# A recurrent attention kernel and its feed-forward: weight loads behind the last crossbar transposes, and the last segment's transposes on TensorE

## The chip, the cores and the metric

The kernel runs on one core of a Trainium2 chip. The time is device microseconds of one launch, as the median of ten runs. Beside the times there is one profiled execution, whose trace all profile lines below are taken from. Engines are called PE (TensorE matmul), PEld (TensorE weight load), DVE (VectorE), ACT (ScalarE), POOL (GpSimd) and SP (SyncE). POOL and SP compute little here: they issue most of the transfers, each in its own order.

## The reference

Two parts follow each other. Part A is attention with a recurrent memory: 2048 tokens in 64 segments of 32, 32 heads of 128, and 8 memory tokens whose output in one segment is the memory of the next. Part B is a gated feed-forward layer on the sum.

```
x = A_x                                   # (1, 2048, 640)
mem = mem0                                # (1, 8, 640)
for s in range(64):
    h = concat([mem, layernorm(x)[segment s]])        # 40 rows
    q, k, v = h @ Wq, h @ Wk, h @ Wv                  # 32 heads x 128
    p = softmax(mask(q k^T * 128**-0.5))              # causal, memory always seen
    o = (p v) @ Wo
    mem, outs[s] = o[:8], o[8:]
h  = x + concat(outs)
n  = layernorm(h)
h2 = h + (relu(n @ W_gate) * (n @ W_up)) @ W_down     # 640 -> 1728 -> 640
```

Because of `mem`, the segments of part A cannot be reordered. In the last segment the memory queries are not needed, since no later segment uses its memory.

## The kernel before, in words

The program is a list of operations, each with its engine, the keys it reads and the keys it writes. `G.solve()` turns keys into semaphore waits; each engine then runs its own operations in the order in which they were added. So the order of the calls is the order of work on every engine, and there is no scheduler. `("Wdone", j)` is written by every projection with weight j (0 for Q, 1 for K, 2 for V), so a load that reads this key starts only after the last such projection.

**A segment.** The loop at L874 runs over s. `project` (L402) multiplies the segment's 32 activations with 4096 columns of a weight in 5 chunks of 128, two halves and four column groups, 40 matmuls of 512 columns. Eight of the 32 columns are the memory; the other 24 are *riders*, tokens of later segments whose keys, queries and values are projected early and kept in the rings Kr, Qr and Vr. A projection arrives with tokens and heads spread over partitions, `to_tok` copies it to bf16 (half on ACT, half on DVE), and a crossbar transpose on SP's queue (`dma_t`, L359) turns it for use: KS (L901) for keys, QS (`trans_q`, L453) for queries. `evac_k` and `evac_q` then copy the riders into the rings, and `v_riders` (L487) moves theirs to Vr with small transfers on POOL's queue. The memory queries alone are needed at once, and TensorE picks them out with eight small matmuls (`pick_mem`, L444).

Then come `scores` (L554), the exponents `exp_mem` and `exp_x` on ACT, the masks on DVE, and the memory rows' product with V (`pv_mem`). `norm_om` and `trans_om` give oT, `wo_pass` (L630) multiplies by Wo in 128 matmuls of 160 columns, and `to_act` puts the new memory into the next segment's activations. This is the recurrence. Between its steps `filler` puts extra riders' projections (`extra_units`, L827) or every fourth segment's collected output rows (`woe_pass`, L643). Segment 1 and segment 62 have neither.

The other 32 rows' output takes a second path: `pv_x` and `norm_x` (L664, L683) write ox, and in the *next* segment `trans_ox` (L693) transposes it by crossbar into oT. Of its rows, 24 share the 32-wide `wo_pass` with the memory of that segment, and 8 are copied to oTe (`copy_oTe`, L697) for `woe_pass`. `rows` and `store_attn` write results to attn_d in memory.

**The seam.** The SBUF of the projection weights W is used again for the feed-forward. In segment 62, right after the Q projection, `load_gate_up` (L815) issues five transfers on POOL: xn2T (the first block's normalised activations), Wg and Wu of 2080 KB each, and two pieces of 80 KB. The last segment leaves the loop after its V projection (L927 to L929). The code from L1050 then issues h and Wd on POOL and eight row loads on SP (`ln2_load`, L713), and mixes segment 63's remaining attention with the first four units of the feed-forward:

```
gate_up(0, 0); scores(s); exp_x(); copy_oTe(s - 1); mask_x()
gate_up(0, 1); pv_x(s, P0); norm_x(P0); wo_pass(T1); rows(T1, 0, s - 1); trans_ox()
gate_up(0, 2); gate_up(0, 3); copy_oTe(s); wo_pass(P2); rows(P2, 1, s); woe_pass(P3, range(16))
```

`gate_up(b, j)` (L995) is one unit: 5 matmuls with Wg and 5 with Wu, 512 tokens wide, relu on ACT, the product on DVE. There are 14 units for each of four blocks, then `down`. From j=5 of block 0 on, DVE also does the layer norm of the next block (`ln2_front`, L718), which needs the rows that SP loaded.

## Time and profile before

| what | value |
|---|---|
| median of ten runs | 1131.71 us (1129.3 to 1138.39) |
| profiled execution | 1133.65 us |
| its span in the trace | 1131.9 us |
| PE busy | 1069.5 us (94%) |
| PEld / DVE / ACT / POOL busy | 509.2 / 592.9 / 352.9 / 288.0 us |
| mean granted PE clock | 0.983 |
| segment 62 | 897.21 to 916.77 us |
| segment 63 and units j=0 to 3 | 916.77 to 955.81 us |
| rest of the feed-forward | 955.81 to 1131.9 us |

The span is the time from the first to the last instruction in the trace. The execution's own time is a little longer, and the median of the ten runs is a little below that execution. In the lines of slices each digit is a fortieth of the span: 9 means 90% busy or more, and in the clock's row 9 is close to full clock. In timelines the first number is the start, the second the duration, then engine, line of the source, operation, output and inputs; in brackets stands how long the engine was idle before and what released it. "To landing" is the time from the issue of a transfer until its data has arrived.

### The profile page before, as it was taken

How to read it: one execution, taken by the hardware profiler on the slowest of the kernel's cores; microseconds unless marked ns; L12 is line 12 of the kernel's file. 1: busy time of each engine (PE TensorE's matmuls, PEld its weight loads, DVE VectorE, ACT ScalarE, POOL GpSimd, SP SyncE). 2: the span in 40 equal slices, each digit the busy share in tenths (PEclk: the TensorE clock that was granted, in tenths of full speed). 3: DMA queues.
4: the chain of work that ended last, by engine and by line, in shares of the span. 5: the costliest groups of instructions: out<-in, count | busy, mean ns of one | idle time of the engine just before them, and what ended most of it. 6: DMA issues, size and time to landing. Idle time of an engine off the chain costs nothing.

```text
span 1131.9 us, 55578 instructions
## 1 busy us (share of the span) xinstructions
PE 1069.5 (94%) x28030; PEld 509.2 (45%) x23471; DVE 592.9 (52%) x1477; ACT 352.9 (31%) x729; POOL 288.0 (25%) x575
## 2 busy tenths in 40 slices
PE   5579999999999999999999999999999958999998
PEld 3344444454444444444444454444444534343443
DVE  3245656565655555666566566555555522553522
ACT  2113333333333333333324333333333311221211
POOL 1013333332323232424242424333332420000000
PEclk9979999999999999999999999999999978999999
DMA  9936464646454455665655666464546484122100
GB/s 354 378 79 109 92 103 88 109 80 110 81 104 89 98 95 99 102 118 112 114 100 115 110 107 101 89 102 84 104 88 103 86 252 123 38 79 73 27 18 24
DMA packets 291880, 122.66 MB, mean 108 GB/s; under 512 B 268064, under 2 KB 281280, under 8 KB 291648
## 3 DMA queue, kind: packets, MB, share of 16 engines
q1 hardware_dynamic: 272272, 95.21, 40.9%
q0 software_dynamic: 19184, 23.89, 9.5%
q8 instruction: 202, 3.31, 1.2%
q14 instruction: 30, 0.25, 0.1%
q10 hardware_dynamic: 192, 0.01, 0.0%
HBM read 36.79 MB, written 7.21 MB: 39 GB/s over the span
## 4 chain that ended last, share of the span: by engine, by line
PE 84%; DMA 8%; DVE 3%; SPq 3%; issue 1%; ACT 0%; DVEq 0%; ACTq 0%
PE ps L419 24%; PE ps L397 23%; PE ps L636 13%; PE ps L1005 10%; PE ps L1038 3%; PE ps L564 3%; PE ps L650 3%; SPq L357 3%; DMA Wo<-in_A_Wo_dram 3%; PE ps L601 3%; DMA QS<-tok 2%; DVE TBf L548 2%; PE ps L448 2%; DMA oT<-ox 1%; DMA Kr<-tok 1%; PE ps L616 1%
## 5 line engine op out<-in xcount | busy, mean ns | idle before, releaser
L419 PE MATMUL ps<-W,act_r 128*32 128x512 bf16 x4277 | 398.5, 386 | 15.2 <-DMA W<-in_A_Wq_dram 3.1
L397 PE MATMUL ps<-W,act_r 128*32 128x512 bf16 x3603 | 353.7, 379 | 0.0
L357 POOL DMA_DIRECT2D Vr<-Vp x376 | 188.4, 508 | 453.0 <-ACT Vp L459 279.5
L419 PEld LDWEIGHTS ps<-W,act_r 128*32 128x32 bf16 x4277 | 117.3, 98 | 274.5 <-issue 214.7
L459 ACT ACTIVATE tok<-ps 128x512 bf16<-128x512 f32 x191 | 110.5, 595 | 253.6 <-PE ps L397 222.9
L636 PE MATMUL ps<-Wo,oT 128*32 128x160 bf16 x8320 | 163.3, 238 | 9.0 <-DMA Wo<-in_A_Wo_dram 7.4
L461 DVE CAST tok<-ps 128x512 bf16<-128x512 f32 x131 | 90.6, 691 | 146.9 <-PE ps L397 121.9
L636 PEld LDWEIGHTS ps<-Wo,oT 128*32 128x32 bf16 x8320 | 148.7, 99 | 35.2 <-DVE oT L461 25.7
L419 PE MATMUL ps<-W,act_e 128*32 128x512 bf16 x900 | 90.5, 381 | 0.0
L397 PE MATMUL ps<-W,act_e 128*32 128x512 bf16 x900 | 90.1, 379 | 0.0
L459 ACT ACTIVATE Qr<-QS 128x512 bf16<-128x512 bf16 (+3 forms) x108 | 70.7, 681 | 52.6 <-DMA QS<-tok 52.4
L689 DVE TENSOR_TENSOR ox<-ps,rx 128x512 bf16<-128x512 f32 x128 | 82.4, 685 | 2.2
L357 POOL DMA_DIRECT2D attn_d<-wtok x64 | 46.7, 729 | 143.0 <-ACT wtok L459 143.0
L548 DVE STREAM_TRANSPOSE TBf<-ps 128x160 f32<-128x160 f32 x64 | 22.4, 350 | 96.5 <-PE ps L636 96.4
L1005 PE MATMUL ps<-xn2T,Wg 128*128 128x512 bf16 x260 | 66.4, 387 | 3.3 <-ACT tok L459 3.3
L1020 DVE TENSOR_TENSOR hT<-g,ps 128x512 bf16<-128x512 bf16 (+1 forms) x56 | 38.5, 687 | 53.7 <-PE ps L1005 49.8
L1005 PE MATMUL ps<-xn2T,Wu 128*128 128x512 bf16 x260 | 66.3, 387 | 0.0
L574 ACT ACTIVATE om<-ps 128x128 bf16<-128x128 f32 x63 | 17.5, 278 | 147.8 <-PE ps L564 147.8
L1038 PE MATMUL ps<-Wd,hT 128*128 128x320 bf16 (+1 forms) x240 | 63.3, 300 | 0.0
L461 DVE CAST Vp<-ps 128x512 bf16<-128x512 f32 x64 | 44.3, 692 | 34.0 <-PE ps L397 23.5
L1018 ACT ACTIVATE g<-ps 128x512 bf16<-128x512 f32 (+1 forms) x56 | 32.5, 593 | 93.4 <-PE ps L1005 93.3
L397 PE MATMUL ps<-Wd,hT 128*128 128x320 bf16 x208 | 56.9, 299 | 0.0
(104 smaller groups left out, 1145.5 us busy)
## 6 DMA issues: line engine op xcount, KB each, us to landing
Vr<-Vp POOLq DMA_DIRECT2D x124, 48.8 KB, 1.9
W<-in_A_Wk_dram SPq DMA_DIRECT2D x2, 2560.0 KB, 13.3
W<-in_A_Wq_dram SPq DMA_DIRECT2D x2, 2560.0 KB, 28.4
W<-in_A_Wv_dram SPq DMA_DIRECT2D x2, 2560.0 KB, 27.4
Wo<-in_A_Wo_dram SPq DMA_DIRECT2D x2, 2560.0 KB, 27.4
xt<-in_A_x_dram SPq DMA_DIRECT2D x30, 160.0 KB, 3.6
Vr<-Vp POOLq DMA_DIRECT2D x128, 32.5 KB, 1.9
attn_d<-wtok POOLq DMA_DIRECT2D x64, 40.0 KB, 2.8
```

The costliest lines, as they stand in the source:

```text
L357: add(eng, lambda e: e.dma_start(dst, src), r=r, w=w, dma=True)
L397: return pe.add_instruction(mybir.InstMatmult(name=nc.get_next_instruction_name(), engine=mybir.EngineType.PE, ins=[pe.lower_ap(rhs), pe.l ...
L419: ins = pe.matmul(*a, start=(c == 0), stop=(c == DC - 1), skip_group_check=True)
L459: add("act", lambda a: a.activation(dst, src, ACTF.Copy), r=r, w=w)
L461: add("dve", lambda v: v.tensor_copy(dst, src), r=r, w=w)
L548: add("dve", lambda v: v.transpose(TBf[:].rearrange("p c t -> p (c t)"), src), r=[wkey], w=[("TBf",)])
L564: i = pe.matmul(bank((P0, P1)[g % 2])[p:p + (M if a else 32), 40 * k:40 * k + 40], lh, Qr[:, h, q, :], start=True, stop=True, skip_group_c ...
L636: i = pe.matmul(bank(bk)[32 * gg:32 * gg + 32, 0:160], oT[:, hb, :], w[:, gg], start=(hb == ORDER[0]), stop=(hb == ORDER[31]), skip_group_ ...
L689: add("dve", lambda v, kh=kh: v.tensor_tensor(ox[:, :, kh, :], src[:, :, kh, 0:128], ap(rx, kh, [[2, 4], [0, 128]]), ALU.mult), r=[B(b0 + ...
L1005: ins = pe.matmul(bank(bk), w[:, c, lo:lo + 128], xn2T[par][:, c, :], start=(c == 0), stop=(c == DC - 1))
L1020: add("dve", lambda v: v.tensor_tensor(hT[par][lo:128, j, :], g1[gi][lo:128, :], bank(bu)[lo:128, :], ALU.mult), r=[B(bu), ("g1", gi)], w= ...
L1038: i = pe.matmul(*a, start=(j == 0), stop=(j == FC - 1), skip_group_check=True)
```

## The change

There are three edits, all between segment 62 and the feed-forward.

1. `load_gate_up` takes a further key. It is called in segment 62 after `copy_oTe(61)` and reads that copy's key, so that POOL waits until the last oT transpose of the loop has landed and been copied. `v_riders` of segment 62 now stands ahead of it on POOL's queue. The row loads and h also read `("Wu",)`.
2. In segment 62 the queries are not transposed by crossbar. `trans8` does eight 128x128 transposes on TensorE, DVE copies the memory queries from PSUM, and ACT the riders' queries.
3. The last segment leaves the loop. Its keys are transposed by `trans8`; ox of segments 62 and 63 by a new `trans_pe` (two groups of four transposes, copied by ACT and DVE), the former into QS, which is free, the latter into oT. The output product of segment 62 reads QS in two halves. The four units `gate_up(0, 0..3)` come after all attention work, and the row loads, h and Wd are issued near the end of it.

```diff
+    def trans_pe(dst, keys):
+        flat = ox[:].rearrange("p k g d -> p (k g d)")
+        for n, (b, eng) in enumerate(((T0, "act"), (T1, "dve"))):
+            def f(pe, n=n, b=b):
+                for k in range(4):
+                    o = 512 * n + 128 * k
+                    ins = pe.matmul(bank_bf(b)[:, k * 128:(k + 1) * 128], flat[:, o:o + 128], ident[:, :],
+                                    is_transpose=True)
+                return ins
+            add("pe", f, r=[("ox", 0), ("ox", 1), ("ident",)], w=[B(b)])
+            copy_op(eng, dst[:, 16 * n:16 * n + 16, :], slots(b, 0, 32)[:, 0:16, :], [B(b)], keys)
...
     def ln2_load(i):
         u = i % 4
-        dma(xt2[u][:, :], x_ap[128 * i:128 * i + 128, :], r=[("Wdone", 1)], w=[("xt2", u)])
-        load_attn(at2[u], i, [("Wdone", 1)], ("at2", u))
+        dma(xt2[u][:, :], x_ap[128 * i:128 * i + 128, :], r=[("Wdone", 1), ("Wu",)], w=[("xt2", u)])
+        load_attn(at2[u], i, [("Wdone", 1), ("Wu",)], ("at2", u))
...
-    def load_gate_up():
-        free = [("Wdone", 0)]
+    def load_gate_up(after):
+        free = [("Wdone", 0)] + after
...
+            if last:
+                break
...
-                if s == NSEG - 2:
-                    load_gate_up()
...
-                if nr:
-                    trans_q()
+            if nr and s < NSEG - 2:
+                trans_q()
             loads()
             project(a, ks, 2, (0, 1), (P2, P3), (0, 1), spare=16)
-            if not last:
+            if s == NSEG - 2:
+                trans8(tok[2], ("tok", 2), tok[3], ("tok", 3), T0)
+                copy_op("dve", Qr[:, :, q, 0:M], slots(T0, 0, M), [B(T0)], [("Qm", q)])
+                evac_q(slots(T0, 0, SEG), B(T0), t0, nr, M, "act")
+            else:
                 pick_mem(T0)
...
             copy_oTe(s - 1)
+        if s == NSEG - 2:
+            load_gate_up([("oTe", (s - 1) % 4)])
         norm_om()
...
+    a, ks = pass_act(s)
+    project(a, ks, 2, (0, 1), (P2, P3), (0, 1))
+    trans8(tok[0], ("tok", 0), tok[1], ("tok", 1), BQ[0])
+    copy_op("dve", KS[:, :, 0:M], slots(BQ[0], 0, M), [B(BQ[0])], [("KS",)])
+    project(a, ks, 2, (0, 1), (P2, P3), (2, 3))
+    scores(s)
+    project(a, ks, 2, (0, 1), (P2, P3), (4,))
+    exp_x()
+    to_v(P3, Vp, 1, ("Vp",), "dve")
+    to_v(P2, Vp, 0, ("Vp",), "act")
+    mask_x()
+    trans_pe(QS, [("QS",)])
+    pv_x(s, P0)
+    copy_op("act", oTe[:, :, M * ((s - 1) % 4):M * ((s - 1) % 4) + M], QS[:, :, 0:M], [("QS",)], [("oTe", (s - 1) % 4)])
+    norm_x(P0)
+    wo_pass(BQ[1], None, QS, [("QS",)], (0,))
+    trans_pe(oT, [("oT", "m"), ("oT", "x")])
+    wo_pass(BQ[1], None, QS, [("QS",)], (1,))
+    rows(BQ[1], 0, s - 1)
+    copy_oTe(s)
+    for i in range(4, 8):
+        ln2_load(i)
+    dma(h_rows[0] <- h_d, waits Wdone 1 and Wu, eng="pool")
+    dma(Wd <- B_W_down, two pieces, waits Wdone 1, eng="pool")
+    wo_pass(BQ[0])
+    rows(BQ[0], 1, s)
     woe_pass(P3, range(16))
     woe_sum(P3)
     woe_store(NSEG // 4 - 1)
+    for j in range(4):
+        gate_up(0, j)
```

The removed lines of the last segment are those quoted in the section on the kernel before. The two `dma(... <- ...)` lines are shortened; the transfers are those of before. `wo_pass` gets arguments for its source, its keys and which of its halves to run.

## The prediction

> **What bounds the kernel now.** I read the slices of the span first.

> ```profile
> PE   5579999999999999999999999999999958999998
> PEclk9979999999999999999999999999999978999999
> ```

> A slice is 28.3 us. TensorE is full from the fifth slice to the end but for slices 33 and 34 (906 to 962 us), where its clock drops too. That is the seam between the last two segments and the feed-forward part, and all edits lie there. The chain of waits over it, merged:

> ```profile
> 903.67 20.67 DMA QS<-tok
> ...
> 927.03 13.65 DMA oT<-ox
> ...
> 943.01 3.94 PE ps L636 x106
> 946.95 4.42 PE ps L1005 x20
> ...
> 955.88 20.61 PE ps L1005 x95
> ```

> Two crossbar transposes hold the end: 34.3 us. From 955.8 on the chain is feed-forward matmuls back to back, and stays so to 1131.9. So the span is the start of the feed-forward's unit j=4 (955.81 in the timeline) plus a tail of 176.1 us. Why the transposes are late shows in POOL's timeline and in the landing times of tile oT, earlier (first landing line, 830 to 900 us) and at the seam (second, 900 to 950 us):

> ```profile
> 902.01 0.59 POOL L357 DMA_DIRECT2D xn2T<-xn_d  x1 [3.11 <-PE ps L397]
> 902.60 0.90 POOL L357 DMA_DIRECT2D Wg<-in_B_W_gate_dram  x1
> 904.32 0.88 POOL L357 DMA_DIRECT2D Wu<-in_B_W_up_dram  x1
> 906.02 2.03 POOL L357 DMA_DIRECT2D Vr<-Vp  x4
> ```
> ```profile
> DMA to landing us min/median/max: 2.8/2.8/2.8
> ```
> ```profile
> DMA to landing us min/median/max: 8.0/10.9/13.7
> ```

> The same transpose lands in 2.8 us when the DMA engines are free and in 8.0 and 13.7 us beside 5 MB of weights. QS, issued at 903.67, took 20.7. The windows show what TensorE does meanwhile (busy time, count; then granted clock, DMA share, GB/s):

> ```profile
> 905.00:910.00 5.00, 0.55 (x16) 0.27 (x16) 0.53 (x3) 1.17 (x3) 3.05 (x6) 0.88 1.06 323
> 910.00:915.00 5.00, 3.44 (x100) 3.17 (x104) 1.95 (x6) 0.00 (x0) 0.00 (x0) 0.50 1.04 320
> 935.00:940.00 5.00, 1.35 (x4) 0.30 (x2) 0.00 (x0) 0.00 (x0) 0.00 (x0) 0.84 1.12 265
> ```

> **Segment 62.** In before it runs from 897.21 to 916.77, where segment 63's first projection starts. Removed: the QS transpose (1 DMA, and 3.51 us of SP's queue). Moved: the five loads of xn2T, Wg, Wu and Wgu, now behind the copy of oT to oTe, behind the four rider DMAs on POOL. Added: eight 128x128 transposes in place of eight 128x32 picks (0.30 us). The opening's transposes took 0.90 us per 16 at full clock, so 0.45: +0.15. ACT's copy of the queries (0.63) moves from behind the QS landing to about 903.1, into ACT's idle time ahead of the exponent at 904.92; nothing is charged, and if it collided it would cost its 0.6. Scores then end at 904.85.

> With no weights in flight the oT transpose, issued at 902.28, lands at 905.1 (2.8), before DVE reaches the copy at about 905.9. Its wait of 4.63 us goes. What is late next is the latency chain exp, mask, memory product, norm, transpose, output product. No filler work exists in segment 62, so I need a segment that also has none: segment 1.

> ```profile
> 74.63 0.28 PE L616 MATMUL ps<-ident,om 128*128 128x128 bf16 x2 [0.73 <-DVE om L609]
> 75.29 3.90 PE L636 MATMUL ps<-Wo,oT 128*32 128x160 bf16 x128 [0.38 <-DVE oT L461]
> 79.86 0.40 PE L419 MATMUL ps<-W,act_r 128*32 128x512 bf16 x4
> ```

> Its scores end at 72.45 and segment 2 starts at 79.86: 7.4 us. So segment 63 starts at S = 904.85 + 7.45 = 912.3 instead of 916.77: 4.5 us won.

> Here the clock matters: that output product took 3.90 us, against 2.32 in a filled segment. [...] I take the row.

> **Segment 63.** Before, it takes 916.77 to 955.81, 39.04 us, of which 8.64 are the units j=0 to 3 (four of 2.16). After, those units follow the attention work, so attention must run with nothing in the gaps. All KS and ox transposes go to TensorE; no DMA is left on the chain. Worked from S:
> K projection 40 matmuls at 0.054, 2.16. DVE's half of the token copy ends at S+3.08 (916.77 to 919.16, plus 0.69); V chunks 0 and 1 (0.86) cover it. Eight transposes 0.45 to S+3.6. KS copy on DVE, 0.2 latency and 0.29, S+4.1, covered by V chunks 2 and 3 to S+4.46; uncovered it would cost 0.5. Scores 0.6, S+5.06. V chunk 4 and the first ox transposes (0.43, 0.45) cover part of exp (0.60, ends S+5.9). DVE's V copy 0.69 ends at S+6.4, the two masks 1.02 (911.83 to 912.85) at S+7.42. Product with V, then DVE's reciprocal at S+8.15 and norm 0.24 + 1.29, S+9.7. The first half of segment 62's output product (half of 2.32) hides there. Transposes 0.45 with 0.05 latency, S+10.2; second half 1.15; segment 63's output product 2.3; the oTe product 2.3: S+15.95. The PSUM copies (a 512-element one: about 0.42 on DVE, between its rows of 0.29 and 0.69 for 256 and 1024; 0.6 on ACT) run beside the second half-product.

> At half clock from S+7.45 to the warm-up, the product, both half-products and the last transposes add 1.85 by the same steps. TensorE is busy some 70% of S+3.6 to S+9.2 against under half in segment 1's gaps, so this is uncertain: between 0 and 1.85 I take 1.2, nearer segment 1. Gate j=0 starts at G = 912.3 + 15.95 + 1.2 = 929.45; segment 63 takes 17.15 without the units against 30.4: 13.25 won.

> **The weights, now later.** POOL waits for the copy (906), but the riders, which wait for ACT's V copy (905.7), occupy it until 907.9, so the added wait costs nothing. The five loads are 5.08 MB; at the 320 GB/s of the windows 15.9 us, so from first bytes near 909.5 to 925.4. Upper end: before's whole duration, 902.01 to 922.8, again from 907.9: 928.7. Both are before Wu is needed at G+1.08. Behind them on POOL stands segment 61's attention store; ACT's copy of wtok for segment 62 must wait for its landing, about 925.5, while due at S+12.5 = 924.8. ACT next frees bank 0 for gate j=0 near 927.6, so this is covered by the oTe product to 929; a landing past 928.5 would move G one for one. The h and Wd loads and SP's eight row loads now wait behind Wu or ACT: 4.1 MB from about 927, 13 us, done by 940. The first row is needed by DVE at j=5 (943), Wd at 960. Before they landed in 7 to 12 us of contention. Instruction fetch beside the weights cost TensorE one stall (0.77 us at 920.1); 0 to 1, inside the range.

> **Sum.** 1131.9 - 4.5 - 13.25 = 1114.15 us of span (929.45 + 8.64 + 176.1 = 1114.2). The profiled execution took 1133.65, 1.75 above its span, and the median is 1131.71, 1.94 below it. The median after: 1114.2 + 1.75 - 1.94 = 1114.0.

> **Rivals.** *Clock stays full* through both segments: 1114.0 - 1.6 - 1.2 = 1111.2. [...]
> *Clock stays low* from the scores of 63 to the gate: about 8.6 us of TensorE work from S+5 on doubles, some 3 of it under DVE's waits: +5.6 in place of 1.2, 1118.4. Against it: after 4 us of work the clock returned at 916.
> *Weights or the store take the place of the transposes.* Wu or the store landing at 932 to 937 would start the gate there: 1116 to 1122. Against it: 320 GB/s held for 15 us and nothing large competes now.
> *Slower:* Wd is now issued after an attention store and h, some 2 us after 926; the first down product, near 960, waits on it. From a landing at 981 on, 54 us after issue, the kernel is slower by 0.3%; against: 11.9 us today.
> *The change does nothing:* only if oT still lands late without the weights; 2.8 us in every earlier segment speaks against.

> **How the numbers follow.** Likeliest case 60%, full clock 15%, low clock 12%, weights or store 8%, slower 4%, nothing 1%. The likeliest alone spans 1112 to 1116.5. The range, 1110.5 to 1119, takes in both clock cases and the first half of the weights case. A measurement tells about 0.3% (3.4 us) from no change: faster 0.95, same 0.01, slower 0.04.

> **What would show it.** Right: no DMA wait over 1 us on the chain between 897 and the gate; segment 63 starting near 912.3; an output product of about 3.9 us in segment 62; POOL's Wg issue near 908.5; the gate near 929.5; a tail of 176 us from j=4. Wrong: TensorE waiting at the gate on Wu, on ACT's wtok copy, or DVE on the attention rows at j=5; or a half clock beyond 920.

## The result, and the profile after

| | before | after |
|---|---|---|
| median | 1131.87 us (1128.3 to 1138.39, 32 runs) | 1118.14 us (1116.44 to 1120.95, 9 runs) |
| after / before | | 0.988, 95% interval 0.9864 to 0.9896 |
| profiled execution, its span | 1133.65, 1131.9 us | 1120.42, 1118.7 us |
| segment 62 starts | 897.21 | 898.49 |
| segment 62 lasts | 19.57 | 13.66 |
| segment 63 to the start of unit j=4 | 39.03 | 30.42 |
| from j=4 to the end | 176.1 | 176.1 |

Forecast were 1114.0 us and a range from 1110.5 to 1119. The kernel is 13.7 us faster where 17.7 were forecast. The time lies inside the range, 4.1 us above the predicted value.

The slices of the kernel after: in slices 33 and 34 TensorE has gone from 5 and 8 tenths to 8 and 8, and the clock from 7 and 8 to 9 and 9.

```profile
PE   4579999999999999999999999999999988999998
PEclk9979999999999999999999999999999999999999
```

The chain of waits of after over the end of segment 63 (start, duration, what it was):

```profile
919.18 0.34 DVE Px L590
919.52 0.04 issue
919.57 0.47 PE ps L674 x19
920.04 0.97 issue
921.01 0.38 PE ps L674 x13
921.40 2.18 PE ps L636 x64
923.58 0.97 PE ps L704 x8
924.55 1.03 PE ps L636 x36
925.58 1.65 issue
927.23 2.40 PE ps L636 x128
929.62 1.62 issue
931.25 0.58 PE ps L636 x21
931.82 2.17 PE ps L650 x64
```

Both crossbar waits of before (20.67 and 13.65 us) are gone, and no DMA stands on the chain from segment 62 to the gate (the first matmul of unit j=0, at 933.93). In their place are three lines "issue" of more than 0.04 us: TensorE stood still for 0.97, 1.65 and 1.62 us, 4.24 in all, and nothing in the program released it. Each breaks off in the middle of one group of matmuls, as TensorE's timeline shows (in brackets the idle time before the line):

```profile
921.01 0.21 PE L674 MATMUL ps<-Vr,Px 64*64 64x129 bf16 x1 [0.97 <-issue]
921.33 2.25 PE L636 MATMUL ps<-Wo,QS 128*32 128x160 bf16 x64
924.48 1.10 PE L636 MATMUL ps<-Wo,QS 128*32 128x160 bf16 x43
927.23 0.58 PE L636 MATMUL ps<-Wo,QS 128*32 128x160 bf16 x21 [1.65 <-issue]
927.59 2.04 PE L636 MATMUL ps<-Wo,oT 128*32 128x160 bf16 x107
931.25 0.58 PE L636 MATMUL ps<-Wo,oT 128*32 128x160 bf16 x21 [1.62 <-issue]
```

After the 19th of 32 matmuls with V, after the 43rd of 64 of a half-product, after the 107th of 128 of a product. Between the first break and the second lie 13 + 64 + 8 + 43 = 128 matmuls, between the second and the third 21 + 107 = 128. Each matmul has its weight load, so the breaks are 256 TensorE instructions apart. The experiments had to settle what this is, and which of the three edits brought the gain.

### The profile page after: what moved, and what is told of

The parts are those of the page before. It is cut to its first block, busy times and chain, and to the rows that moved or that the text cites. A ratio compares the mean times of both kernels' runs of the same rounds, so it can differ in the third digit from the quotient of the medians.

```text
span 1118.7 us, 55631 instructions
## 1 busy us (share of the span) xinstructions
PE 1063.2 (95%) x28054; PEld 507.0 (45%) x23495; DVE 593.6 (53%) x1479; ACT 354.8 (32%) x732; POOL 287.6 (26%) x575
## 4 chain that ended last, share of the span: by engine, by line
PE 86%; DMA 6%; DVE 4%; SPq 3%; issue 1%; ACT 0%; DVEq 0%
PE ps L419 24%; PE ps L397 23%; PE ps L636 13%; PE ps L1021 10%; PE ps L650 3%; PE ps L564 3%; PE ps L1054 3%; DMA Kr<-tok 3%; SPq L357 3%; DMA Wo<-in_A_Wo_dram 3%; PE ps L601 3%; DVE TBf L548 2%; PE ps L448 2%; PE ps L616 1%; DVE act_r L549 1%
## 5 line engine op out<-in xcount | busy, mean ns | idle before, releaser
L419 PE MATMUL ps<-W,act_r 128*32 128x512 bf16 x4277 | 394.1, 383 | 14.7 <-DMA W<-in_A_Wq_dram 3.0
L397 PE MATMUL ps<-W,act_r 128*32 128x512 bf16 x3603 | 352.6, 379 | 0.1
L357 POOL DMA_DIRECT2D Vr<-Vp x376 | 188.2, 508 | 465.3 <-ACT Vp L459 293.2
L419 PEld LDWEIGHTS ps<-W,act_r 128*32 128x32 bf16 x4277 | 114.8, 97 | 273.2 <-issue 214.1
L636 PE MATMUL ps<-Wo,oT 128*32 128x160 bf16 x8192 | 158.2, 235 | 13.4 <-DMA Wo<-in_A_Wo_dram 9.0
L461 DVE CAST tok<-ps 128x512 bf16<-128x512 f32 x131 | 90.6, 691 | 148.6 <-PE ps L397 117.5
L636 PEld LDWEIGHTS ps<-Wo,oT 128*32 128x32 bf16 x8192 | 143.6, 98 | 39.3 <-DVE oT L461 24.8
L419 PE MATMUL ps<-W,act_e 128*32 128x512 bf16 x900 | 90.6, 381 | 0.0
L397 PE MATMUL ps<-W,act_e 128*32 128x512 bf16 x900 | 90.2, 379 | 0.0
L357 POOL DMA_DIRECT2D attn_d<-wtok x64 | 46.8, 731 | 116.2 <-ACT wtok L459 116.2
L461 DVE CAST Vp<-ps 128x512 bf16<-128x512 f32 x64 | 44.3, 692 | 31.4 <-PE ps L397 26.2
L397 PE MATMUL ps<-Wd,hT 128*128 128x320 bf16 x208 | 56.9, 299 | 0.0
```

Source lines behind the costliest of these rows:

```text
L357: add(eng, lambda e: e.dma_start(dst, src), r=r, w=w, dma=True)
L397: return pe.add_instruction(mybir.InstMatmult(name=nc.get_next_instruction_name(), engine=mybir.EngineType.PE, ins=[pe.lower_ap(rhs), pe.l ...
L419: ins = pe.matmul(*a, start=(c == 0), stop=(c == DC - 1), skip_group_check=True)
L461: add("dve", lambda v: v.tensor_copy(dst, src), r=r, w=w)
L636: i = pe.matmul(bank(bk)[32 * gg:32 * gg + 32, 0:160], src[:, hb, :], w[:, gg], start=(hb == ORDER[0]), stop=(hb == ORDER[31]), skip_group ...
```

## The experiments

Ratios are to the kernel before on the same chip; the kernel before had medians of 1131.4, 1134.0 and 1135.4 us on the three chips used, so totals are compared by ratio, not by their microseconds. Times of segments and stops are from the profiled execution of each run. Segment 62 began anywhere from 895.4 to 900.1 us in these profiles, before any of the edits acts on the chain, so the stretches from segment 62 or 63 to unit j=4 tell more of the edits than the totals do. A table at the end of this section has them for every run.

### Which edit brings the gain

`e1_defer_only` is the kernel before with edit 1 alone, `e2_first_two` with edits 1 and 2:

```diff
 # e1
-                if s == NSEG - 2:
-                    load_gate_up()
...
+        if s == NSEG - 2:
+            load_gate_up([("oTe", (s - 1) % 4)])
 # e2, in addition
+            if s == NSEG - 2:
+                trans8(tok[2], ("tok", 2), tok[3], ("tok", 3), T0)
+                copy_op("dve", Qr[:, :, q, 0:M], slots(T0, 0, M), [B(T0)], [("Qm", q)])
+                evac_q(slots(T0, 0, SEG), B(T0), t0, nr, M, "act")
...
```

> The kernel before with the first edit alone: the weight loads wait for the copy of oT, all crossbar transposes and the old order of the last segment stay. If edits add up as the prediction counted them, only segment 62's stall goes: about 1127 (4.5 less than 1131.9). Theory: gate j=0 stands ahead of segment 63's scores on TensorE and now waits for Wu near 926, as late as before, but segment 63's oT transpose is issued some 10 us earlier and lands with the weights near 926 to 930 instead of 941: 1119 to 1126. Rival: the transposes of segment 63 meet the weights, then h, Wd and the rows, and oT lands near 940 again: 1130 to 1133, no change.

> The first and the second edit together, the last segment as before. Theory: with the weights deferred the crossbar transpose of the queries lands in about 5 us anyway, so the second edit gives nothing beside the first: within 1 us of the run with the first alone. Rival: it was QS that held ACT and all behind it, so that the second edit gives 3 us or more over the first alone.

Measured: e1 1130.84 us, ratio 0.9952 (0.9924 to 0.9981); e2 1133.21, 0.9979 (0.9959 to 0.9998). By its microseconds e1 seems to meet the rival of no change, but its chip was slow: before took 1135.36 there. By the ratio it gained 0.2 to 0.8% (2 to 9 us), and the count of 4.5 us for the first edit lies inside that. The theory that oT of segment 63 would land with the weights and bring more fell: in the run's trace that transpose took 20.9 us. Segment 62 was shortened by 6.2 us in e1 and by 4.5 in e2 (from 19.57 to 13.40 and 15.10 us), and part of it was given back behind it (segment 63 to j=4: 41.68 and 39.63 us, before 39.03), so that 3.5 and 3.9 us are left in the profiles. What gives it back is the next crossbar transpose, that of segment 63's keys. From the chains of waits of e1 and then of e2:

```profile
915.28 21.50 DMA KS<-tok
```
```profile
917.34 19.18 DMA KS<-tok
```

Transposes of keys took 3.0 to 3.2 us in earlier segments of before. Weights that start later are in flight later: the transposes of segment 62 are free of them, and those of segment 63 meet them. Edit 2 adds nothing to edit 1 that these runs resolve. The opposite experiment, `e10_no_defer`, is the kernel after with the weights issued where before has them, behind segment 62's Q projection:

```diff
             project(a, ks, 0, (0, 1), (P0, P1), spare=40)
+            if s == NSEG - 2:
+                load_gate_up([])
...
-        if s == NSEG - 2:
-            load_gate_up([("oTe", (s - 1) % 4)])
```

> The changed kernel with the first edit undone: the weights are issued right after segment 62's Q projection again, the other two edits stay. Theory: only segment 62's oT transpose is left on the crossbar beside the weights and lands in 8 us instead of 2.8, so segment 63 starts some 4.5 us later than in the changed kernel; the weights are then down by 922, before segment 63's products, and the first two stalls for instructions (2.6 us) go: 1120 to 1123. Rival: the riders' transfers behind the weights (10 us landing) hold segment 63's V copy or product as well: 1125. Rival: the first edit does nothing: 1118.

Measured: 1119.66 us, ratio 0.9881 (0.9852 to 0.9911), beside 1119.52 and 0.9871 (0.9844 to 0.9897) for the kernel after on the same chip. So edits 2 and 3 bring nearly the whole gain without the first (edit 2 added nothing to e1; edit 3 was not run alone). In the totals the weights' place makes no difference that these runs resolve (some 3 us). The profiles still show one: from segment 62 to j=4, e10 takes 45.87 us, after 44.08 and 42.80 (e12). They also show why it is small. Without the deferral segment 62 takes 17.79 us against 13.85 in the run of after beside it, because the oT transpose lands in 6.3 us (TensorE waits 2.57 us ahead of the transposes of `om` instead of 0.73) and the product behind ran at half clock (4.46 us instead of 2.40). But in segment 63 TensorE stops for only 0.26 and 0.59 us, instead of for 2.71 (e12). Against that stands a new wait: the riders' transfers take 14.9 us (median) beside the weights, and DVE's copy of V waits for them. The timelines of TensorE and then of DVE in e10:

```profile
916.58 0.39 PE L419 MATMUL ps<-W,act_r 128*32 128x512 bf16 x2 [0.26 <-issue]
930.52 0.57 PE L636 MATMUL ps<-Wo,oT 128*32 128x160 bf16 x21 [0.59 <-issue]
```
```profile
921.07 0.69 DVE L461 CAST Vp<-ps 128x512 bf16<-128x512 f32 x1 [2.57 <-DMA Vr<-Vp]
```

### What the stops are

The profile of after lists a DMA queue named "instruction" that moved 202 packets. The author's guess was that it brings TensorE's instructions in blocks of 256, and that each stop is a wait for the next block. The timeline of after alone does not show this. To ask whether the bulk loads make the difference, `e3_light_weights` loads one of the five row chunks of Wg and Wu and multiplies with it five times (four chunks' weights are left out, the work is not), and `e4_late_loads` keeps h, Wd and the eight row loads back until the first feed-forward unit is done:

```diff
 # e3
-            dma(t[:, :, :], src.rearrange(...)[:, :, 0:FM],
+            dma(t[:, 0:1, :], src.rearrange(...)[:, 0:1, 0:FM],
...
-                    ins = pe.matmul(bank(bk), w[:, c, lo:lo + 128], xn2T
+                    ins = pe.matmul(bank(bk), w[:, c if w is Wgu else 0, lo:lo + 128], xn2T
 # e4: the loads stand behind the gate_up loop, each with one key more
+        [("hT", 0, 0)]
```

> The changed kernel with one of the five chunks of Wg and Wu loaded, and that chunk used in place of all five (the feed-forward's values are those of other weights; matmuls, sizes and order are the same). Theory: TensorE's three stalls without a releaser in segment 63 (0.97, 1.65, 1.62 us at 920, 925.6, 929.6), which stand 128 matmul and load pairs apart, are waits for instructions whose fetch competes with the transfers. With 3.4 MB less in flight the first two shrink below 0.5 each, the third stays: 1116 and no gate wait. Rival: the fetch takes this long by itself: all three stay, 1118. Rival: the stalls are hidden waits on weights: all go, 1114.

> The changed kernel with the eight row loads, h and Wd issued only after the product of unit j=0. Theory of fetch beside transfers: the third stall (1.62 us at 929.6, between the issue of h, Wd and rows and the end of the oTe product) shrinks below 0.5, the first two stay: 1116.6. Rival (the fetch's own length): the third stall stays, 1118. The rows then land some 10 us later; if DVE waits on them at j=5, the time is over 1118.

Measured: e3 1116.22 us, ratio 0.9824 (0.9798 to 0.985); e4 1118.89, 0.9856 (0.9822 to 0.989). In e3's timeline the first stop is gone, the second shrank from 1.65 to 0.89, the third stayed:

```profile
925.91 0.57 PE L636 MATMUL ps<-Wo,QS 128*32 128x160 bf16 x21 [0.89 <-issue]
929.93 0.57 PE L636 MATMUL ps<-Wo,oT 128*32 128x160 bf16 x21 [1.62 <-issue]
```

In e4 the second stop grew to 2.44 us and the third vanished, but the product that had held it ran at half clock, so that nothing was won from segment 63 to the gate (21.74 us, after 21.78). E4's timeline:

```profile
925.10 0.83 PE L636 MATMUL ps<-Wo,QS 128*32 128x160 bf16 x21 [2.44 <-issue]
925.62 4.08 PE L636 MATMUL ps<-Wo,oT 128*32 128x160 bf16 x128
```

A product with the third stop, 2.40 + 1.62 = 4.02 us, and one at half clock without it, 4.08, cost the same. One caution: the kernel after, unchanged, was profiled once more (`e12_after_again`, below) and there too the first stop was absent, the second was long (2.71 us) and the product behind it ran at half clock without a third. So of e3 and e4 only the short second stop of e3 can be put down to the edit. Next the boundary was moved. `e5_shift40` puts 40 more weight loads into segment 63's projections, where TensorE is busy anyhow; `e8_warm_fill` puts six 512-wide matmuls of no use (12 instructions) where TensorE waits for the masks, to keep the clock up:

```diff
 # e5, in segment 63
-            project(a, ks, 1, (0, 1), BQ, spare=40)
+            project(a, ks, 1, (0, 1), BQ, spare=40, more=20 if last else 0)
...   the three V projections likewise: more=8, 8, 4
 # e8
     trans_pe(QS, [("QS",)])
+    for n in range(6):
+        pe.matmul(bank(BQ[0]), ident[:, :], W[:, 2, n % 5, 0:512], start=True, stop=True)
     pv_x(s, P0)
```

> The changed kernel with 40 more weight loads in segment 63's projections (the same 32-column weights loaded again where they were kept), which wide matmuls cover. Theory of instruction lines: the boundaries lie 256 TensorE instructions apart, so each stall comes 20 pairs earlier: the first just ahead of the product with V, where TensorE waits 1.2 us for the masks anyway, the second after some 23 pairs of the second half-product, the third after some 87 pairs of segment 63's product. The first stall's 0.97 us is hidden: 1117. Rival (stalls belong to places or transfers, not to counts): stalls after the same matmuls as before, 1118 to 1119.

> The changed kernel with six dummy 128x512 matmuls into a free bank while TensorE waits for the masks of segment 63 (1.2 us). Theory: the half clock from 921.3 to 924.6 follows from low activity since 918; with the gap filled the clock stays up, the first half-product takes 1.1 instead of 2.2 us and the transposes 0.5 instead of 0.97, of which about 1 us is on the chain: 1117.1. Rival: the 0.97 us stall behind it is what lowers the clock: no change, 1118; the dummies may also push the product with V by up to 0.3.

Measured: e5 1119.05 us, ratio 0.9882 (0.9858 to 0.9906); e8 1116.83, 0.986 (0.9837 to 0.9883). First e5's timeline, then e8's:

```profile
920.19 0.59 PE L636 MATMUL ps<-Wo,QS 128*32 128x160 bf16 x23
923.81 0.92 PE L636 MATMUL ps<-Wo,QS 128*32 128x160 bf16 x41 [3.03 <-issue]
924.52 4.07 PE L636 MATMUL ps<-Wo,oT 128*32 128x160 bf16 x128
```
```profile
918.80 1.29 PE L636 MATMUL ps<-Wo,QS 128*32 128x160 bf16 x64
920.99 0.86 PE L636 MATMUL ps<-Wo,QS 128*32 128x160 bf16 x37
924.13 1.12 PE L636 MATMUL ps<-Wo,QS 128*32 128x160 bf16 x27 [2.28 <-issue]
```

The stop moves by exactly the instructions put in: 40 of them are 20 pairs, and it stands after 43 - 20 = 23 matmuls; 12 are 6 pairs, and it stands after 43 - 6 = 37. So it is tied to the count of instructions, not to a tile, a bank or a moment. Moving it doesn't remove it, and e5's forecast of a faster kernel failed. In e8 the first half-product ran at full clock (1.29 us against 2.25 in after), and the stop behind it was longer. The filling matmuls need not be the cause of that clock: the half-product took 1.29 us in e3, e4, e5 and e12 too, without them.

The remaining test takes instructions away. `e7_wide_products` computes the last two output products in 64 matmuls of 320 columns instead of 128 of 160 (their results lie in two halves of partitions, which one ACT copy and one DVE addition join); `e6_mixed_units` leaves the products and puts the four feed-forward units between them, as before had it:

```diff
 # e7
+                    ins = pe.matmul(bank(bk)[32 * q:32 * q + 32, 0:320], src[:, hb, :],
+                                    w[:, 2 * (q % 2):2 * (q % 2) + 2], start=(i == 0), stop=(i == 15), ...
...
-    wo_pass(BQ[0])
+    wide_pass(BQ[0], oT, [("oT", "m"), ("oT", "x")], range(16))
 # e6
+    gate_up(0, 0)
     wo_pass(BQ[1], None, QS, [("QS",)], (1,))
...
-    wo_pass(BQ[0]); rows(BQ[0], 1, s)
+    gate_up(0, 1)
+    wo_pass(P2); rows(P2, 1, s)
+    gate_up(0, 2)
     woe_pass(P3, range(16))
...
-    for j in range(4):
-        gate_up(0, j)
+    gate_up(0, 3)
```

> The changed kernel with the output products of segments 62 and 63 as 64 matmuls of 320 columns in place of 128 of 160 (two halves of the heads side by side, added by ACT and DVE afterwards): the same columns streamed, half the instructions. Theory of instruction lines: lines last twice as long there, the second and third stall go: 1115. Rival (transfers or clock): TensorE is as long as before, 1118.

> The changed kernel with units j=0 to 3 put between the attention products again: j=0 ahead of the second half-product, j=1 behind it, j=2 behind segment 63's product, j=3 last. A unit takes 2.16 us with 20 instructions, a product 2.3 us with 256. Theory: a line then lasts longer than its fetch, the second and third stall (3.3 us) go, and j=0 waits at most 0.5 us for Wu: 1115. Rival (the stalls are fetch of a fixed place or other): 1118. Rival: j=0 waits for Wu to 928 and holds all behind it: 1118 to 1120.

Measured: e7 1115.31 us, ratio 0.9848 (0.9826 to 0.987); e6 1116.92, 0.986 (0.9838 to 0.9883). In both the second and third stop are gone; the first, in the product with V, stayed (1.55 and 1.82 us). From segment 63 to j=4, e7 takes 26.93 us and e6 27.65, against 30.42 and 28.95 in the two profiles of after. The totals do not resolve this: their intervals touch that of after (0.9864 to 0.9896). E7's timeline, with the wide products at the line of the new helper:

```profile
921.47 0.26 PE L675 MATMUL ps<-Vr,Px 64*64 64x129 bf16 x1 [1.55 <-issue]
924.80 1.27 PE L1073 MATMUL ps<-Wo,QS 128*32 128x320 bf16 x32
925.89 2.35 PE L1073 MATMUL ps<-Wo,oT 128*32 128x320 bf16 x64
```

The queue list of the page names the fetches themselves (packets, MB, share of the DMA engines' time), first in after, then in e7:

```profile
q8 instruction: 202, 3.31, 1.2%
```
```profile
q8 instruction: 201, 3.29, 1.2%
```

After has 28054 matmuls and 23495 weight loads on TensorE; divided by 256 that is 201.4, and 202 packets were moved. E7 has 256 instructions fewer (27926 and 23367), and one packet fewer. So this queue carries TensorE's instructions, one packet for 256 of them, and as TensorE enters a new block, a packet follows. The start of each packet, beside TensorE's times:

| run, block | TensorE enters the block before it | packet starts | TensorE goes on | in all | transfers from entry to packet |
|---|---|---|---|---|---|
| after, second | 921.01 | 924.68 | 927.23 | 6.2 | 346 GB/s, DMA share 0.90 |
| e12, second | 920.87 | 924.61 | 927.08 | 6.2 | 399 GB/s, 1.01 |
| e4, second | 919.16 | 922.66 | 925.10 | 5.9 | 366 GB/s, 0.94 |
| e3, second | 921.51 | 923.66 | 925.91 | 4.4 | 258 GB/s, 0.96 |
| after, third | 927.23 | 928.85 | 931.25 | 4.0 | 277 GB/s, 0.91 |
| e3, third | 925.91 | 927.66 | 929.93 | 4.0 | 4 GB/s, 0.01 |

Windows like these of after show the transfers (busy time and count of PE, PEld, DVE, ACT and POOL, then clock, DMA share, GB/s):

```profile
922.00:923.00 1.00, 1.00 (x40) 1.00 (x36) 0.96 (x2) 0.00 (x0) 0.00 (x0) 0.50 1.03 413
926.00:927.00 1.00, 0.00 (x0) 0.00 (x0) 0.00 (x0) 0.00 (x0) 0.00 (x0) 1.00 0.01 2
928.00:929.00 1.00, 1.00 (x72) 1.00 (x64) 0.00 (x0) 0.14 (x1) 0.56 (x1) 1.00 0.89 281
```

In these six blocks 4.0 to 6.2 us pass from a block's first matmul until the next block can run. The last stretch, from the packet to TensorE's start, is 2.3 to 2.6 us in all of them, even where nothing else moves (the middle window, inside the second stop). What differs is the time until the packet starts: 1.6 to 1.8 us in the third blocks, 3.5 to 3.7 in the second ones of after, e12 and e4. Taking four fifths of Wg and Wu away brought the second block's down to 2.2 (e3, one profile), so it is these transfers that lengthen it. The DMA share doesn't tell the cases apart (0.90 with 3.7 us, 0.91 with 1.6); the rate does, 346 GB/s and more against 277 and less.

At full clock, 128 matmuls of 160 columns with their loads use a block up in 2.40 us. Hence 4.02 - 2.40 = 1.62 for the third stop. Hence also why full clock did not help e8 and half clock did not hurt e4: e8's first half-product at full clock was followed by a longer stop (2.28 us against 1.65 in after), and a product took 4.02 us at full clock with the third stop in after and 4.08 at half clock without it in e4. The request for a block is not in the trace; that it goes out on entering the block before is read from these intervals. It can go out ahead of the matmul that begins the block: in e10, where TensorE entered the last block at half clock and without a stop, only 3.0 us passed (927.48 to 930.52), with the packet at 928.19 and the same 2.3 us behind it.

### Both together, and once more after

`e11_wide_warm` joins e7 and e8, `e9_mixed_wide` joins e6 and e7, and `e12_after_again` is the kernel after, unchanged, on the same chip.

> Wide products and the gap ahead of the product with V filled with six dummy matmuls. Theory: the wide form removes the second and third stall, so that no long stall lowers the clock again, and the fill keeps the clock up for the first half-product: 1113. Rival: the stall in the product with V stays (1.5 us) and takes the fill's gain: 1115.

> Units mixed between the products and the products wide, both at once. If the second and third stall are one cause that each of the two removes, they don't add: 1115 to 1116, as with either alone. If each removes something else, 1112.

> The changed kernel once more beside these. Expected 1118; stalls without a releaser after the same three matmuls as in its first profile if they belong to the instruction count, of other lengths if they depend on what is in flight; segment 62's product at full or at half clock (2.4 or 3.9 us), if that hangs on the moment.

Measured: e11 1115.52 us, ratio 0.9845 (0.9817 to 0.9872); e9 1119.29, 0.987 (0.9844 to 0.9897); e12 1119.52, 0.9871 (0.9844 to 0.9897). E11's only stop:

```profile
923.92 1.52 PE L1073 MATMUL ps<-Wo,oT 128*32 128x320 bf16 x37
925.80 1.13 PE L1073 MATMUL ps<-Wo,oT 128*32 128x320 bf16 x27 [0.37 <-issue]
```

It stands after 37 of 64 wide matmuls, where the count of 128 pairs puts it. From the start of segment 62 to j=4 e11 takes 40.23 us; after took 44.08 and, in e12, 42.80. It is the fastest of the versions in its profile, and its median is 4.0 us below that of after on the same chip, though the two intervals overlap by 0.0028. E9's total was a miss (1115 to 1116 was expected). With both edits the first feed-forward unit comes so early that it waits for its weights. That is not what made the total long: from segment 63 to j=4 the profile takes 26.24 us, less than e6 or e7, but its segment 62 began at 900.14, later than in any other profile; why is open. E9's list of waits (us in all, times, longest):

```profile
PE ps L1023 <- DMA Wu<-in_B_W_up_dram: 1.2, 1, 1.2
```

E12 repeats the stop after 43 matmuls, with another length: it has no first stop and its half-product ran at full clock, so its wait for a block that again took 6.2 us began earlier:

```profile
923.43 0.94 PE L636 MATMUL ps<-Wo,QS 128*32 128x160 bf16 x43
927.08 0.96 PE L636 MATMUL ps<-Wo,QS 128*32 128x160 bf16 x21 [2.71 <-issue]
927.73 3.68 PE L636 MATMUL ps<-Wo,oT 128*32 128x160 bf16 x128
```

All profiles over the stretch that the edits touch, in us. After and e12 are one kernel, so a difference of less than some 1.5 us from segment 63 to j=4 is not resolved by one profile each.

| run | segment 62 | segment 63 to j=4 | both |
|---|---|---|---|
| before | 19.57 | 39.03 | 58.60 |
| e1, first edit | 13.40 | 41.68 | 55.08 |
| e2, first two | 15.10 | 39.63 | 54.73 |
| after | 13.66 | 30.42 | 44.08 |
| e12, after again | 13.85 | 28.95 | 42.80 |
| e10, no deferral | 17.79 | 28.08 | 45.87 |
| e3, light weights | 15.19 | 27.40 | 42.59 |
| e4, late loads | 13.66 | 30.16 | 43.82 |
| e5, 40 instructions more | 13.66 | 29.96 | 43.62 |
| e8, filled gap | 15.30 | 28.59 | 43.89 |
| e6, mixed units | 15.20 | 27.65 | 42.85 |
| e7, wide products | 15.16 | 26.93 | 42.09 |
| e9, mixed and wide | 15.77 | 26.24 | 42.01 |
| e11, wide and filled | 15.08 | 25.15 | 40.23 |

## Why the prediction was right, and where it was not

**The bound and the transposes: right.** Removing the crossbar from the chain ended both waits. oT's transpose in segment 62 landed in 2.9 us (2.8 predicted), and the tail from j=4 is 175.9 to 176.1 us in every kernel that was run.

**Segment 63's steps up to the product with V: right.** It was due 7.42 us after the segment's start and began there: 912.15 + 7.42 = 919.57.

**Weights and loads: right.** Wg was issued at 910.05 instead of near 908.5, and Wu landed at 911.80 + 14.2 = 926.0 (925.4 predicted), well before the gate at 933.93. The rivals of a wait for weights, for the store or for Wd did not come; in e9, whose first unit starts at 926.26, the first of them does.

**The term that was mis-sized** is "Instruction fetch beside the weights cost TensorE one stall (0.77 us at 920.1); 0 to 1, inside the range." It entered the sum with nothing. It measured 4.24 us in the profile of after, and 2.71 in e12, where a product at half clock took the place of the third stop. It was priced as one event, from a stop of before that stood among 512-wide matmuls (first line). What sets its price is how fast a stretch uses instructions up, and edit 3 made such a stretch: 128 narrow matmuls for each of two output products, one behind the other. Before, 20 wide feed-forward matmuls of 4.4 us stood between these products, and the last of them ran in 2.40 us without a stop (second line):

```profile
920.10 0.39 PE L419 MATMUL ps<-W,act_r 128*32 128x512 bf16 x2 [0.77 <-issue]
951.31 2.40 PE L636 MATMUL ps<-Wo,oT 128*32 128x160 bf16 x128
```

The prediction counted the units' move to the end as free of cost; they had been the cover of the fetch. The mechanism was on the list, and its size was off.

**The clock: half right, and decided by luck.** For segment 62's product the row of segment 1, 3.90 us, was taken over the 2.32 of a filled segment; their difference is the 1.6 of the rival with a full clock. After took 2.40, and segment 62 ended 1.44 us sooner than its term. But with the same idle gaps ahead (0.75, 0.73 and 0.40 us) the product ran at full clock in the profiles of after, e1, e4, e5 and e12, and at half clock (3.6 to 4.0 us) in e2, e3, e6, e7, e8, e9 and e11. The traces show what tells them apart. In the profiles of before and after the half clock was granted in stretches of 3.41, 6.83 and 10.24 us, one to three times 3.41, all on one grid in each profile; in before it began at 908.79 and 925.86, in after at 921.45, which is another place on a grid of 3.41 us. Two windows of the grid each, first of after, then of e6; the product began in the second of each pair:

```profile
904.38:907.80 3.42, 2.52 (x105) 1.55 (x116) 2.01 (x7) 1.85 (x4) 0.31 (x1) 1.00 0.30 68
907.80:911.21 3.41, 2.43 (x132) 2.26 (x136) 1.72 (x5) 0.00 (x0) 3.41 (x7) 1.00 0.34 54
```
```profile
904.34:907.75 3.41, 1.69 (x96) 1.03 (x88) 2.10 (x7) 1.25 (x3) 1.41 (x3) 1.00 0.06 15
907.75:911.16 3.41, 3.25 (x100) 3.25 (x104) 1.04 (x3) 0.00 (x0) 3.41 (x6) 0.50 0.55 137
```

In after the gaps were split between two windows, 0.90 and 0.98 us of TensorE's idle time in each. In e6 one window held 1.72 us of it, and the next was at half clock. So it is in all twelve profiles with these gaps (e10's differ): the five with full clock have at most 1.58 us idle in one window here, the seven with half clock 1.60 to 1.88. The edge is not sharp (windows with 1.62, 1.65 and 1.73 us were followed by full clock elsewhere in after and e5), and no run was made to test it. By this reading the place of the gaps on the grid, which nothing in the program sets, decided on these 1.4 us.

In segment 63 the clock was at half from 921.45 to 924.86 us, behind a window with 2.13 us of idle time: 1.16 of waiting for the masks and the first stop, 0.97. In e12, without that stop, 1.26 us were idle there and the clock stayed full. The first half-product and the transposes behind it took 1.4 us longer than in e12, near the 1.2 that was charged; but behind them stood a fetch that would not have come sooner. The half clock behind the second stop in e4, e5 and e12 follows windows with 2.1 to 2.6 us idle. The rivals of a clock full or low throughout did not come in the profile of after.

**The sum.** From segment 63 to the gate: 21.78 us instead of 17.15, +4.63. Segment 62: 13.66 instead of 15.1, -1.44. Segment 62 began 1.28 us later than in the profile of before; in the other profiles it began at 895.4 to 900.1, so this is put down to no edit. Together +4.5, which is the miss on the span, 1118.7 against 1114.15.

**A right total by two errors of opposite sign.** The prediction gave 4.5 us of gain to segment 62, and the profile shows 5.9, of which 1.4 is the clock's luck. It gave 13.25 to segment 63, and the profile shows 8.61. With segment 62's product at half clock, as in seven of twelve profiles, the span would have missed by an estimated 6 us (4.5 + 1.4) instead of 4.5. The deferral's own share stays rough: alone it brought 0.2 to 0.8% (e1), and beside the other edits 1.8 to 3.1 us by the profiles and nothing that the totals resolve (e10). Part of what segment 62 gains is lost again, since the weights that it sends into segment 63 slow the fetch there: a block took 6.2 us in after and e12, and 4.4 in e3, which loads a fifth of Wg and Wu.

## What to carry to other kernels

Count instructions, not only time: in this kernel short matmuls used up 256 TensorE instructions in 2.40 us, at full clock, where the next block took 4.0 to come (5.9 to 6.2 beside weight transfers of 346 to 399 GB/s), so TensorE waited for its own instructions, and the profile shows it as "issue" in the middle of a group, 256 instructions apart. Fewer and wider matmuls, or long ones put between, removed the stops in the products here; a faster clock or moving the boundary did not. The weights that were deferred off one latency chain landed on the next (in e1 the keys' transpose took 21.50 us beside them, 3.0 to 3.2 in earlier segments of before): look for what a deferred transfer will lie beside.
